# A fused attention and two feed-forward layers: a first-layer result written over its operand, buffers dealt out again, and a new order

## The chip, the core and the metric

The kernel runs on one core of a Trainium2 chip. A core has a matrix engine (TensorE, PE in the profile, with its weight loads as PEld), VectorE (DVE), ScalarE (ACT), GpSimd (POOL) and SyncE (SP), which issues the DMAs. Each engine works through its own queue in order; engines wait for one another by semaphores. The metric is the device time of one execution, in microseconds.

## The reference

`x` is 2 x 12480 x 128, float32. An attention step takes each batch through 32 inducing points; two feed-forward layers without biases follow, each 128 -> 2048 -> 128, over all 24960 tokens:

```
def mab(q, kv): a = softmax(scale * q @ kv.T); return a @ kv
h = mab(inducing, x);  x = mab(x, h)                 # per batch
h = x @ w_in1                                        # first layer
P = a0 + a1*h + a2*h^2 + a3*h^3
Q = 1 + |b0|*|h| + |b1|*h^2
x = (P / (Q + 1e-6)) @ w_out1
h = x @ w_in2                                        # second layer
out = (h * cos(h)) @ w_out2
```

## The kernel before

A first stretch computes the attention weights of both batches, turns the weights to float32, and multiplies the 32 attended rows `h` with `w_in1` (`mst`, `m3`, `m1`), so that the first layer's first product can be had from the attention weights themselves. Then come 52 blocks of 480 tokens. A block has eight first-layer tiles of 256 hidden units, in two halves of 480 columns each, and sixteen second-layer halves of 128 hidden units.

One first-layer tile (`moe1_tile`) goes through these steps; the letters are the names in the code. Per half: `mmA` (TensorE, L847 with `mst`) gives h in a PSUM bank, `sq` (L853) and `ab` (L856) on ScalarE read it, and free the bank. Per tile: `wq` (L859) and `qq` (L862) on GpSimd form Q, `ln` (L865) and `ex` (L868) on ScalarE its inverse, and `ee` (L871) on GpSimd the factor of a Newton step. Per half again: `mmX` (L847 with `m3`), `n1` (L877, VectorE), `mmY` (L847 with `m1`), `gr` (L885, VectorE), `ng` (L890, VectorE), which ends the use of the bank, and `mmB` (L895), which adds the result into `acc[0]`. After a block's last `mmB` one instruction of ScalarE, L951, copies the sum to `xt`: its 52 starts mark the blocks.

A second-layer half (`moe2_tile`) is `mmC` (L978) into a bank, `rk` (L981, ScalarE), `rd` (L984, VectorE), `sn` (L987, ScalarE, a sine), `gg` (L990, VectorE), which frees the bank, and `mmD` (L993) into `acc[1]`. Sine and logarithm need different function tables on ScalarE: L1073 loads one, twice in a block.

Six PSUM banks serve both layers; `hc` limits how many of them the second layer holds. Tiles in SBUF are buffers of kinds `x1` to `x6`, each kind with its own count; one `x1` and one `x2` more lie in the two `wide` tiles. In the first layer `x1` holds |h|, then Q, then `ee`'s result; `x2` holds `wq`, then the inverse; `x3` holds the square; `x4` holds `ng`'s result for `mmB`. The weights are staged in `x4` as they come from DRAM, before the blocks begin.

The order of all engines' queues is made at build time by `Plan.order`: a list scheduler with a cost for each operation (the numbers in `mop(...)`), a number of buffers for each kind, and a due time from the tables `OFF` and `START` (`START` for the first two blocks). An operation that takes a buffer (`acq`) is not placed before an earlier one has given it back (`rel`). On the chip only the order stands; the waits are semaphores.

Of the kernel before, what the change touches and what calls it, by code (L numbers as in the profile page):

```python
# [24 lines left out]


TUNE = {
    "NX": {"x1": 5, "x2": 5, "x3": 5, "x4": 4, "x5": 5, "x6": 6, "hc": 4},
    "PARTS": 1,
    "ADDED": (0, 1, 2, 3, 4, 5, 6, 7),  # L30
    "OFF": {
        "slope1": 0.92, "slope2": 0.28, "shift2": -238.65, "hi": 417.72, "lo": 468.96, "tr": 485.58, "cp": -316.77,
        "kA": 478.1, "kX": 444.49, "kC": -311.86, "mmA": -443.25, "mmX": 423.28, "mmY": 174.81, "mmB": 432.98,
# [3 lines left out]
    },  # L37
    "START": {
        "slope1": 1.67, "slope2": 0.77, "shift2": 13.3, "hi": 39.19, "lo": 476.68, "tr": 416.75, "cp": 442.76,
        "kA": -405.75, "kX": 125.03, "kC": 0.0, "mmA": -197.73, "mmX": 475.77, "mmY": 104.53, "mmB": 57.46,  # L40
        "mmC": 0.0, "mmD": 10.0, "sq": 494.18, "ab": -357.19, "ln": 522.15, "ex": 488.76, "rk": -20.0, "sn": -30.0,
        "wq": -10.71, "qq": 120.95, "ee": 494.63, "wb": -96.93, "n0": 95.71, "n1": -280.16, "gr": 25.55, "ng": 67.25,
        "rd": 0.0, "gg": -10.0, "cpx": 420.38,
    },
}

# [209 lines left out]
def kernel(  # L256
# [13 lines left out]
    NB, N, C = x.shape  # L270
# [7 lines left out]
    TB = G * TP  # L278
# [8 lines left out]
    NX = {k: n for k, n in TUNE["NX"].items() if k != "hc"}  # L287
# [23 lines left out]
    wout1 = const.tile([128, DFF], F32, name="wout1")  # L311
# [12 lines left out]
    acc = [psum.tile([128, 512], F32, name=f"acc{i}") for i in range(2)]  # L324
# [13 lines left out]
    M = {}  # L338
# [103 lines left out]
    def plan_weights(w, out, dst, prio):  # L442

        ends = []
        for f in range(0, DFF, 384):
            n = min(384, DFF - f)
            c, d = {}, {}

            def load(c=c, f=f, n=n):
                raw = M["x4"][c["x4"]][:, 0:2 * n].bitcast(I32)  # L450
                if out:
                    nc.sync.dma_start(out=raw.rearrange("p (k d w) -> p k d w", d=C, w=2), in_=bits_out(w)[:, f // C:(f + n) // C])
                else:
                    nc.sync.dma_start(out=raw.rearrange("p (n w) -> p n w", w=2), in_=bits_in(w)[:, f:f + n, :])

            def tiles(c=c, d=d, n=n):
                raw = M["x4"][c["x4"]][:, 0:2 * n].bitcast(I32).rearrange("p (n w) -> p n w", w=2)
                t = M["x1"][d["x1"]]
                return raw, t[:, 0:n], t[:, n:2 * n]

            ends.append((f, n, plan_narrow(
                n, load, tiles, lambda f=f, n=n: dst[:, f:f + n], prio + 0.05 * len(ends), [],
                acq=[("x4", c, False), ("x1", d, False)], rel=[("x4", c), ("x1", d)],
            )))
        return ends
# [271 lines left out]
    products = {}  # L737
# [47 lines left out]
    def mop(*a, **k):  # L785
        return op(*a, main=True, **k)
# [37 lines left out]
    def moe1_tile(blk, k):  # L824

        b = blk // NQ
        blkd = blocks[blk]
        at = blkd["c"]
        c, ca, cx = {}, [{}, {}], [{}, {}]
        ac = blkd.setdefault("acc1", {})  # L830
# [12 lines left out]
        def hf(kind, h):  # L843
            return fl(kind)[:, h * TB:(h + 1) * TB]
# [4 lines left out]
        def mmA(h):  # L849
            return mm(ca[h], mst, h, start=True, stop=True)  # L850
# [48 lines left out]

# [25 lines left out]
        ng_ = []  # L925
        for h in range(2):
            oX = mop(
                "pe", 205, lambda h=h: mmX(h), [oe, *again, *([blkd["rX"][k]] if h else [])], pri("mmX", h) - 1e5, lock=cx[h],
                acq=[("half", cx[h], False), *([] if h else [("x4", c, True)])], key=pri("kX"),
            )  # L930
            o8 = mop("dve", 600, lambda h=h: n1(h), [oX], pri("n1", h), rel=[("x3", c)] if h else [], lock=cx[h])
            oY = mop("pe", 205, lambda h=h: mmY(h), [o8, *([blkd["rY"][k]] if h else []), blkd.get("Y")], pri("mmY", h) - 1e5, lock=cx[h],
                     rel=[("at", at)] if h and last else [])
            blkd["rX"][k], blkd["rY"][k] = oX, oY
            if h:
                blkd["Y"] = oY
            o9 = mop("dve", 600, lambda h=h: gr(h), [oY, *ng_], pri("gr", h), lock=cx[h], rel=[("x2", c)] if h else [])
            o9 = mop("dve", 600, lambda h=h: ng(h), [o9, o6, *ng_], pri("ng", h), lock=cx[h],
                     rel=[("half", cx[h]), *([("x1", c)] if h else [])])
            ng_ = [o9]  # L940
            prev = mop(
                "pe", 805, lambda h=h: mmB(h), [o9, prev, *within(wout1_ends, 256 * k, 256)], pri("mmB", h),
                acq=[("accB", ac, True)] if k == 0 and h == 0 else [], rel=[("x4", c)] if h else [],
            )
        blkd["B"].append(prev)
        n2_ = prev
# [8 lines left out]
    def moe2_tile(blk, k, h):  # L955
# [154 lines left out]
```

## Time and profile before

| | |
|---|---|
| median of 3 runs | 3115.25 us (3109.82 to 3116.71) |
| profiled execution, its own time | 3111.72 us |
| its span, first to last instruction | 3109.9 us |
| mean granted TensorE clock | 0.966 of full speed |
| busy share: PE, ACT, DVE, POOL | 92%, 90%, 86%, 75% |
| DMA | 48.7 MB, nearly all of it in the first 240 us |

The profile is one execution. A share of the span is a mean over the first stretch and 52 blocks; the blocks are most of it, so that they are read one by one. A duration in a row is from start to end of one instruction; instructions that follow at once overlap a little, so that the start of one to the start of the next is the shorter and better measure of what it costs its engine. An idle time in brackets is that of the engine just before the instruction, with what ended it.

### The profile page before, as it was taken

What the parts mean: (1) busy time and instruction counts of PE and PEld (TensorE: products, weight loads), DVE (VectorE), ACT (ScalarE), POOL (GpSimd) and SP (SyncE); (2) the same over time, 40 slices, a digit from 0 to 9 for tenths busy, and PEclk for the clock granted to TensorE, in tenths of its full rate; (3) what the DMA queues carried; (4) which work ended last, traced back from release to release, by engine and by line L of the source; (5) the groups of instructions that cost most, each with busy time, mean ns of one, the idle gap of its engine ahead of it and who ended that gap; (6) DMA issues with size and microseconds to landing.
All of it is one profiled execution on the core that took longest, in us unless ns stands there. A gap on an engine that the chain in (4) does not pass through costs nothing.

```text
span 3109.9 us, 30950 instructions
## 1 busy us (share of the span) xinstructions
PE 2863.5 (92%) x8903; PEld 1500.0 (48%) x8903; DVE 2676.3 (86%) x4492; ACT 2791.4 (90%) x4701; POOL 2322.5 (75%) x1320
## 2 busy tenths in 40 slices
PE   6669999999999999999998999999989999999998
PEld 3334454554545455454444454544444545455454
DVE  4978898988989888898888898989788989898897
ACT  3558999999999999999899999999898999999995
POOL 0268878787887878878768778787787887878772
PEclk8769999999999999999999999999999999999999
DMA  8420000000000000000000000000000000000000
GB/s 221 141 78 4 4 4 7 4 7 4 7 4 4 7 4 7 4 7 4 4 7 4 4 7 4 4 7 4 7 4 4 7 4 7 4 4 7 4 7 7
DMA packets 27583, 48.73 MB, mean 16 GB/s; under 512 B 3028, under 2 KB 7412, under 8 KB 27412
## 3 DMA queue, kind: packets, MB, share of 16 engines
q1 hardware_dynamic: 27412, 46.76, 5.3%
q8 instruction: 70, 1.15, 0.2%
q14 instruction: 101, 0.83, 0.1%
HBM read 33.97 MB, written 12.78 MB: 15 GB/s over the span
## 4 chain that ended last, share of the span: by engine, by line
PE 35%; ACT 24%; POOL 22%; issue 9%; DVE 8%; DMA 2%; SPq 0%; ACTq 0%; DVEq 0%; POOLq 0%
PE bank L978 15%; PE acc L993 10%; POOL x L871 8%; POOL x L862 7%; PE bank L847 5%; POOL x L859 4%; ACT x L865 4%; PE acc L895 4%; ACT x L868 3%; ACT x L853 3%; ACT x L987 3%; ACT x L856 3%; ACT L1073 2%; ACT x L981 2%; DVE x L890 2%
## 5 line engine op out<-in xcount | busy, mean ns | idle before, releaser
L871 POOL TENSOR_TENSOR x<-x,x 128x960 f32<-128x960 f32 x348 | 779.4, 2246 | 316.6 <-ACT x L868 316.6
L847 PE MATMUL bank<-at,m 128*128 128x480 f32 x1664 | 822.6, 544 | 52.5 <-DVE bank L877 26.7
L895 PE MATMUL acc<-x,wout 128*128 128x480 f32 x1664 | 810.4, 585 | 3.8 <-DVE x L890 2.0
L862 POOL TENSOR_TENSOR x<-x,x 128x960 f32<-128x960 f32 x348 | 781.8, 2252 | 6.5 <-ACT x L856 1.0
L978 PE MATMUL bank<-xt,wt 128*128 128x480 f32 x1664 | 745.5, 578 | 37.9 <-ACT x L856 32.0
L993 PE MATMUL acc<-x,wt 128*128 128x480 f32 x1664 | 770.3, 566 | 0.0
L984 DVE TENSOR_TENSOR x<-x,bank 128x480 f32<-128x480 int32 x832 | 526.5, 649 | 207.2 <-ACT x L981 203.9
L877 DVE SCALAR_TENSOR_TENSOR bank<-bank,par,x 128x480 f32<-128x480 f32 x832 | 580.8, 720 | 55.6 <-PE bank L847 53.8
L859 POOL TENSOR_SCALAR x<-x,babs 128x960 f32<-128x960 f32 x348 | 373.9, 1078 | 313.9 <-ACT x L853 273.7
L981 ACT ACTIVATE x<-bank 128x480 int32<-128x480 f32 x832 | 479.2, 581 | 98.3 <-PE bank L978 94.6
L853 ACT ACTIVATE x<-bank 128x480 f32<-128x480 f32 x832 | 463.8, 590 | 69.3 <-PE bank L847 68.6
L990 DVE TENSOR_TENSOR x<-x,bank 128x480 f32<-128x480 f32 x832 | 512.8, 648 | 6.5 <-ACT x L987 2.4
L847 PEld LDWEIGHTS bank<-at,m 128*128 128x128 f32 x1664 | 309.1, 190 | 433.5 <-DVE bank L877 220.9
L885 DVE SCALAR_TENSOR_TENSOR bank<-bank,par,x 128x480 f32<-128x480 f32 x696 | 490.6, 720 | 26.6 <-PE bank L847 25.0
L847 PE MATMUL bank<-at,mst 128*128 128x480 f32 x832 | 414.1, 547 | 94.3 <-DVE x L890 87.9
L978 PEld LDWEIGHTS bank<-xt,wt 128*128 128x128 f32 x1664 | 313.9, 194 | 385.3 <-issue 149.5
L890 DVE SCALAR_TENSOR_TENSOR x<-x,bank 128x480 f32<-128x480 f32 x696 | 443.4, 649 | 61.1 <-POOL x L871 52.5
L987 ACT ACTIVATE x<-x 128x480 f32<-128x480 f32 x832 | 465.9, 602 | 31.0 <-DVE x L984 28.7
L856 ACT ACTIVATE x<-bank,babs 128x480 f32<-128x480 f32 x696 | 458.5, 697 | 0.0
L895 PEld LDWEIGHTS acc<-x,wout 128*128 128x128 f32 x1664 | 316.2, 194 | 161.0 <-issue 115.6
L993 PEld LDWEIGHTS acc<-x,wt 128*128 128x128 f32 x1664 | 311.8, 189 | 161.2 <-issue 139.7
L865 ACT ACTIVATE x<-x 128x960 f32<-128x960 f32 x348 | 360.8, 1048 | 9.7 <-POOL x L862 8.9
(116 smaller groups left out, 2214.7 us busy)
## 6 DMA issues: line engine op xcount, KB each, us to landing
wide<-in_x_dram SPq DMA_DIRECT2D x75, 240.0 KB, 4.4
out_dram<-on SPq DMA_DIRECT2D x52, 240.0 KB, 2.4
x<-in_x_dram SPq DMA_DIRECT2D x29, 240.0 KB, 7.3
x<-in_moe_w_out_dram SPq DMA_DIRECT2D x10, 384.0 KB, 5.0
x<-in_moe_w_in_dram SPq DMA_DIRECT2D x10, 384.0 KB, 5.3
x<-in_moe_w_out_dram SPq DMA_DIRECT2D x2, 128.0 KB, 4.6
x<-in_moe_w_in_dram SPq DMA_DIRECT2D x2, 128.0 KB, 2.8
ind<-in_inducing_dram SPq DMA_DIRECT2D x1, 16.0 KB, 1.5
```

The lines of the kernel that those rows point to most:

```text
L847: return nc.tensor.matmul(out=ps(e), lhsT=m[k][:, h * 128:(h + 1) * 128], rhs=M["at"][at["at"]], **flags)
L853: nc.scalar.activation(out=hf("x3", h), in_=ps(ca[h]), func=AF.Square)
L856: nc.scalar.activation(out=hf("x1", h), in_=ps(ca[h]), func=AF.Abs, scale=babs[:, 0:1])
L862: nc.gpsimd.tensor_tensor(out=fl("x1"), in0=fl("x2"), in1=fl("x1"), op=ALU.add)
L871: nc.gpsimd.tensor_tensor(out=fl("x1"), in0=fl("x1"), in1=fl("x2"), op=ALU.mult)
L877: nc.vector.scalar_tensor_tensor(out=ps(cx[h]), in0=ps(cx[h]), scalar=par[:, 2:3], in1=hf("x3", h), op0=ALU.add, op1=ALU.mult)
L895: nc.tensor.matmul(out=acc[0][:, 0:TB], lhsT=wout1[:, (2 * k + h) * C:(2 * k + h + 1) * C], rhs=hf("x4", h), start=(k == 0 and h == 0), st ...
L978: return nc.tensor.matmul(out=ps(), lhsT=win2[:, f * 128:(f + 1) * 128], rhs=M["xt"][xc["xt"]], start=True, stop=True)
L981: nc.scalar.activation(out=fl("x5").bitcast(I32), in_=ps(), func=AF.Identity, bias=0.25)
L984: nc.vector.tensor_tensor(out=fl("x5"), in0=fl("x5").bitcast(I32), in1=ps(), op=ALU.subtract)
L987: nc.scalar.activation(out=fl("x5"), in_=fl("x5"), func=AF.Sin, scale=-TWO_PI, bias=0.5 * math.pi)
L993: nc.tensor.matmul(out=acc[1][:, 0:TB], lhsT=wout2[:, f * C:(f + 1) * C], rhs=fl("x6"), start=first, stop=last)
```

## The change

`ng` writes its result over its operand in `x1`; `mmB` reads it there, and `x1` is given back by the second `mmB`, no longer by the second `ng`. `x4` is gone. Its four buffers become two more of `x1` (5 to 7), one of `x2` (5 to 6) and one of `x3` (5 to 6); `hc` goes from 4 to 5. The weights are staged in `x3`. `x2` is taken by `wq` on GpSimd, no longer by `mmA` on TensorE. The planner's costs are set anew, and with them nearly all entries of `OFF` and `START`, of which two lines stand here:

```diff
-    "NX": {"x1": 5, "x2": 5, "x3": 5, "x4": 4, "x5": 5, "x6": 6, "hc": 4},
+    "NX": {"x1": 7, "x2": 6, "x3": 6, "x5": 5, "x6": 6, "hc": 5},
...
-                raw = M["x4"][c["x4"]][:, 0:2 * n].bitcast(I32)
+                raw = M["x3"][c["x3"]][:, 0:2 * n].bitcast(I32)
...
 def ng(h):
-                out=hf("x4", h), in0=hf("x1", h), scalar=-2.0, in1=ps(cx[h]), op0=ALU.add, op1=ALU.mult
+                out=hf("x1", h), in0=hf("x1", h), scalar=-2.0, in1=ps(cx[h]), op0=ALU.add, op1=ALU.mult
 def mmB(h):
-                out=acc[0][:, 0:TB], lhsT=wout1[:, (2 * k + h) * C:(2 * k + h + 1) * C], rhs=hf("x4", h),
+                out=acc[0][:, 0:TB], lhsT=wout1[:, (2 * k + h) * C:(2 * k + h + 1) * C], rhs=hf("x1", h),
...
 # costs: mmA, mmX, mmY 205 -> 213; mmB, mmC, mmD 805 -> 820; n1, gr 600 -> 630; ng 600 -> 570
-                acq=[("half", ca[h], False), *([] if h else [("x1", c, True), ("x2", c, True), ("x3", c, True)])], key=pri("kA"),
+                acq=[("half", ca[h], False), *([] if h else [("x1", c, True), ("x3", c, True)])], key=pri("kA"),
...
-        o3 = mop("pool", 961, wq, sqs, pri("wq"))
+        o3 = mop("pool", 961, wq, sqs, pri("wq"), acq=[("x2", c, True)], key=pri("kA"))
...
-                acq=[("half", cx[h], False), *([] if h else [("x4", c, True)])], key=pri("kX"),
+                acq=[("half", cx[h], False)],
...
-                     rel=[("half", cx[h]), *([("x1", c)] if h else [])])
+                     rel=[("half", cx[h])])
...
-                acq=[("accB", ac, True)] if k == 0 and h == 0 else [], rel=[("x4", c)] if h else [],
+                acq=[("accB", ac, True)] if k == 0 and h == 0 else [], rel=[("x1", c)] if h else [],
```

The work is the same, 6067 instructions of TensorE, 4494 of VectorE, 4689 of ScalarE and 1325 of GpSimd by the built programs' rows; only their order and buffers differ. In both orders a pattern of one block repeats. Before, the order of ScalarE is line for line that of the block ahead in 24 of 50 pairs of neighbouring blocks; after, in 40.

On TensorE, in the middle of a block before, second-layer products (L978, L993) stand among the first layer's (`mst` is `mmA`, `m_76` to `m_83` are `mmX`, `m_84` to `m_91` are `mmY`, `wout` is `mmB`):

```order
L978 MATMUL bank<-xt_137,wt_66 128x480 x2
L847 MATMUL bank<-at_134,m_4_80 128x480
L895 MATMUL acc_97<-x_0_117,wout_67 128x480
L847 MATMUL bank<-at_134,m_4_80 128x480
L895 MATMUL acc_97<-x_0_117,wout_67 128x480
L847 MATMUL bank<-at_134,m_4_88 128x480 x2
L847 MATMUL bank<-at_135,mst_69 128x480
L895 MATMUL acc_97<-x_3_120,wout_67 128x480
L847 MATMUL bank<-at_135,mst_69 128x480
L895 MATMUL acc_97<-x_3_120,wout_67 128x480
L978 MATMUL bank<-xt_137,wt_66 128x480 x4
```

On TensorE after, in the stretch of a block that has most of the second layer; five L978 and the four transposes of L806 stand just ahead of these rows:

```order
L993 MATMUL acc_98<-x_2_128,wt_66 128x480
L978 MATMUL bank<-xt_136,wt_66 128x480 x5
L993 MATMUL acc_98<-x_3_129,wt_66 128x480
L993 MATMUL acc_98<-x_4_130,wt_66 128x480
L993 MATMUL acc_98<-x_5_131,wt_66 128x480
L993 MATMUL acc_98<-x_0_126,wt_66 128x480
L993 MATMUL acc_98<-x_1_127,wt_66 128x480
L993 MATMUL acc_98<-x_2_128,wt_66 128x480
L993 MATMUL acc_98<-x_3_129,wt_66 128x480
L993 MATMUL acc_98<-x_4_130,wt_66 128x480
L993 MATMUL acc_98<-x_5_131,wt_66 128x480
L847 MATMUL bank<-at_134,m_0_76 128x480 x2
```

What moved: 11 of the 16 L978 of a block and 11 of its 16 L993 now stand together, with no first-layer product among them, and the rest of the block is nearly all first layer.

On GpSimd, in a block before (`x_102` to `x_106` and `wide_132` are `x1`, `x_107` to `x_111` and `wide_133` are `x2`, `x_112` to `x_116` are `x3`; L859 is `wq`, L862 `qq`, L871 `ee`):

```order
L859 TENSOR_SCALAR x_3_110<-x_0_112,babs 128x960
L859 TENSOR_SCALAR x_4_111<-x_1_113,babs 128x960
L862 TENSOR_TENSOR x_2_104<-x_3_110,x_2_104 128x960
L862 TENSOR_TENSOR x_4_106<-x_4_111,x_4_106 128x960
L859 TENSOR_SCALAR x_0_107<-x_2_114,babs 128x960
L871 TENSOR_TENSOR wide_132<-wide_132,wide_133 128x960
L862 TENSOR_TENSOR x_3_105<-x_0_107,x_3_105 128x960
L859 TENSOR_SCALAR x_1_108<-x_3_115,babs 128x960
L871 TENSOR_TENSOR x_1_103<-x_1_103,x_2_109 128x960
L862 TENSOR_TENSOR x_0_102<-x_1_108,x_0_102 128x960
L871 TENSOR_TENSOR x_2_104<-x_2_104,x_3_110 128x960
```

On GpSimd after, in a block's second half (`x_102` to `x_108` and `wide_132` are `x1`, `x_109` to `x_114` and `wide_133` are `x2`, `x_115` to `x_120` are `x3`):

```order
L801 TENSOR_TENSOR pk_138<-att_92,pk_138 120x8x32
L871 TENSOR_TENSOR x_0_102<-x_0_102,wide_133 128x960
L871 TENSOR_TENSOR x_4_106<-x_4_106,x_3_112 128x960
L871 TENSOR_TENSOR x_5_107<-x_5_107,x_4_113 128x960
L871 TENSOR_TENSOR x_6_108<-x_6_108,x_1_110 128x960
L859 TENSOR_SCALAR x_0_109<-x_4_119,babs 128x960
L859 TENSOR_SCALAR wide_133<-x_5_120,babs 128x960
L862 TENSOR_TENSOR x_1_103<-x_0_109,x_1_103 128x960
L871 TENSOR_TENSOR x_2_104<-x_2_104,x_5_114 128x960
L862 TENSOR_TENSOR wide_132<-wide_133,wide_132 128x960
L859 TENSOR_SCALAR x_3_112<-x_3_118,babs 128x960
L871 TENSOR_TENSOR x_3_105<-x_3_105,x_2_111 128x960
```

What moved: of the eight L871 of a block, four now stand in one row with no L862 between them; before, at most two did, and two L862 stood ahead of single ones. 160 of the 416 L859 now wait for VectorE, where 91 did.

## Rows read from the trace of the kernel before

**Rows 1.** The page, part 1: busy us, share of the span, number of instructions.

```profile
PE 2863.5 (92%) x8903; PEld 1500.0 (48%) x8903; DVE 2676.3 (86%) x4492; ACT 2791.4 (90%) x4701; POOL 2322.5 (75%) x1320
```

**Rows 2.** Instructions of line 951: durations, first and last start.

```profile
L951 ACT ACTIVATE xt<-acc x52: 571/682/708, 243.4 to 3076.9; 128x480 f32<-128x480 f32 x52
```

**Rows 3.** Timeline of ScalarE: start us, us, line, operation; six of the 52.

```profile
418.27 0.71 ACT L951 ACTIVATE xt<-acc 128x480 f32<-128x480 f32 x1
688.01 0.68 ACT L951 ACTIVATE xt<-acc 128x480 f32<-128x480 f32 x1
1344.29 0.68 ACT L951 ACTIVATE xt<-acc 128x480 f32<-128x480 f32 x1
1698.52 0.68 ACT L951 ACTIVATE xt<-acc 128x480 f32<-128x480 f32 x1
2027.52 0.68 ACT L951 ACTIVATE xt<-acc 128x480 f32<-128x480 f32 x1
2428.16 0.70 ACT L951 ACTIVATE xt<-acc 128x480 f32<-128x480 f32 x1
```

**Rows 4.** Busy time by engine in four stretches (columns in the first line).

```profile
core 0: us, PE busy (x) PEld busy (x) DVE busy (x) ACT busy (x) POOL busy (x), PEclk, DMA share, GB/s
418.30:688.00 269.70, 256.95 (x762) 135.85 (x762) 242.20 (x401) 259.82 (x435) 221.28 (x126) 1.00 0.02 5
489.50:526.10 36.60, 36.60 (x114) 20.08 (x112) 34.78 (x59) 34.72 (x62) 26.97 (x16) 1.00 0.03 7
688.00:743.80 55.80, 53.11 (x154) 27.78 (x152) 48.42 (x81) 52.21 (x89) 44.37 (x26) 0.97 0.02 5
705.50:708.90 3.40, 3.40 (x6) 1.55 (x5) 1.86 (x4) 2.13 (x6) 3.40 (x2) 0.50 0.00 0
```

**Rows 5.** Timelines in one block: idle time and its releaser in brackets.

```profile
481.69 1.88 PE L978 MATMUL bank<-xt,wt 128*128 128x480 f32 x4 [0.74 <-ACT x L856]
487.85 0.48 PE L847 MATMUL bank<-at,mst 128*128 128x480 f32 x1 [1.74 <-DVE x L890]
...
481.70 0.66 DVE L890 SCALAR_TENSOR_TENSOR x<-x,bank 128x480 f32<-128x480 f32 x1 [1.73 <-POOL x L871]
...
476.20 2.24 POOL L862 TENSOR_TENSOR x<-x,x 128x960 f32<-128x960 f32 x1
479.44 2.22 POOL L871 TENSOR_TENSOR x<-x,x 128x960 f32<-128x960 f32 x1
...
474.60 0.99 ACT L868 ACTIVATE x<-x 128x960 f32<-128x960 f32 x1
```

**Rows 6.** Timelines of ScalarE and TensorE: instructions that follow one another at once.

```profile
480.05 1.05 ACT L853 ACTIVATE x<-bank 128x480 f32<-128x480 f32 x2
480.95 1.25 ACT L856 ACTIVATE x<-bank,babs 128x480 f32<-128x480 f32 x2
482.03 1.05 ACT L865 ACTIVATE x<-x 128x960 f32<-128x960 f32 x1
...
506.97 1.59 ACT L987 ACTIVATE x<-x 128x480 f32<-128x480 f32 x3
508.57 1.28 ACT L1073 ACT_TABLE_LOAD   x1
509.87 1.90 ACT L865 ACTIVATE x<-x 128x960 f32<-128x960 f32 x2
511.67 1.89 ACT L868 ACTIVATE x<-x 128x960 f32<-128x960 f32 x2
...
490.30 3.38 PE L978 MATMUL bank<-xt,wt 128*128 128x480 f32 x8
```

**Rows 7.** The page, part 5: groups of instructions.

```profile
L984 DVE TENSOR_TENSOR x<-x,bank 128x480 f32<-128x480 int32 x832 | 526.5, 649 | 207.2 <-ACT x L981 203.9
L877 DVE SCALAR_TENSOR_TENSOR bank<-bank,par,x 128x480 f32<-128x480 f32 x832 | 580.8, 720 | 55.6 <-PE bank L847 53.8
L981 ACT ACTIVATE x<-bank 128x480 int32<-128x480 f32 x832 | 479.2, 581 | 98.3 <-PE bank L978 94.6
```

More of the change, by code (lines that the diff above doesn't have):

```diff
@@ L31 @@
     "OFF": {
-        "slope1": 0.92, "slope2": 0.28, "shift2": -238.65, "hi": 417.72, "lo": 468.96, "tr": 485.58, "cp": -316.77,
-        "kA": 478.1, "kX": 444.49, "kC": -311.86, "mmA": -443.25, "mmX": 423.28, "mmY": 174.81, "mmB": 432.98,
[3 rows of a table removed]
+        "slope1": 0.22, "slope2": 1.13, "shift2": -299.88, "hi": -115.8, "lo": 225.65, "tr": 141.68, "cp": -305.88,
+        "kA": 166.97, "kX": 126.25, "kC": 41.99, "mmA": -91.5, "mmX": 84.49, "mmY": -112.0, "mmB": 415.69,
[3 rows of a table added]
     },
     "START": {
[L39 to L43, printed above, removed]
+        "slope1": 2.42, "slope2": 0.77, "shift2": 13.3, "hi": -268.77, "lo": 278.33, "tr": 53.48, "cp": 50.66,
+        "kA": -204.51, "kX": 102.37, "kC": 0.0, "mmA": -74.63, "mmX": 487.87, "mmY": 141.02, "mmB": 251.0, "mmC": 0.0,
+        "mmD": 10.0, "sq": -289.58, "ab": 199.42, "ln": -89.18, "ex": 151.14, "rk": -20.0, "sn": -30.0, "wq": -687.43,
+        "qq": -122.84, "ee": 279.42, "wb": -96.93, "n0": 95.71, "n1": -84.36, "gr": 66.2, "ng": -739.77, "rd": 0.0,
+        "gg": -10.0, "cpx": 277.38,
     },
@@ L456, in tiles @@
             def tiles(c=c, d=d, n=n):
-                raw = M["x4"][c["x4"]][:, 0:2 * n].bitcast(I32).rearrange("p (n w) -> p n w", w=2)
+                raw = M["x3"][c["x3"]][:, 0:2 * n].bitcast(I32).rearrange("p (n w) -> p n w", w=2)
                 t = M["x1"][d["x1"]]
@@ L462, in plan_weights @@
                 n, load, tiles, lambda f=f, n=n: dst[:, f:f + n], prio + 0.05 * len(ends), [],
-                acq=[("x4", c, False), ("x1", d, False)], rel=[("x4", c), ("x1", d)],
+                acq=[("x3", c, False), ("x1", d, False)], rel=[("x3", c), ("x1", d)],
             )))
@@ L908, in moe1_tile @@
             o = blkd["A"] = mop(
-                "pe", 205, lambda h=h: mmA(h), [blkd["at"], *products[b, k], blkd.get("A"), *(full if blk > 1 else [])],
+                "pe", 213, lambda h=h: mmA(h), [blkd["at"], *products[b, k], blkd.get("A"), *(full if blk > 1 else [])],
                 pri("mmA", h) - 1e5, lock=ca[h],
-                acq=[("half", ca[h], False), *([] if h else [("x1", c, True), ("x2", c, True), ("x3", c, True)])], key=pri("kA"),
+                acq=[("half", ca[h], False), *([] if h else [("x1", c, True), ("x3", c, True)])], key=pri("kA"),
             )
@@ L927, in moe1_tile @@
             oX = mop(
-                "pe", 205, lambda h=h: mmX(h), [oe, *again, *([blkd["rX"][k]] if h else [])], pri("mmX", h) - 1e5, lock=cx[h],
-                acq=[("half", cx[h], False), *([] if h else [("x4", c, True)])], key=pri("kX"),
-            )
-            o8 = mop("dve", 600, lambda h=h: n1(h), [oX], pri("n1", h), rel=[("x3", c)] if h else [], lock=cx[h])
-            oY = mop("pe", 205, lambda h=h: mmY(h), [o8, *([blkd["rY"][k]] if h else []), blkd.get("Y")], pri("mmY", h) - 1e5, lock=cx[h],
+                "pe", 213, lambda h=h: mmX(h), [oe, *again, *([blkd["rX"][k]] if h else [])], pri("mmX", h) - 1e5, lock=cx[h],
+                acq=[("half", cx[h], False)],
+            )
+            o8 = mop("dve", 630, lambda h=h: n1(h), [oX], pri("n1", h), rel=[("x3", c)] if h else [], lock=cx[h])
+            oY = mop("pe", 213, lambda h=h: mmY(h), [o8, *([blkd["rY"][k]] if h else []), blkd.get("Y")], pri("mmY", h) - 1e5, lock=cx[h],
                      rel=[("at", at)] if h and last else [])
@@ L936, in moe1_tile @@
                 blkd["Y"] = oY
-            o9 = mop("dve", 600, lambda h=h: gr(h), [oY, *ng_], pri("gr", h), lock=cx[h], rel=[("x2", c)] if h else [])
-            o9 = mop("dve", 600, lambda h=h: ng(h), [o9, o6, *ng_], pri("ng", h), lock=cx[h],
-                     rel=[("half", cx[h]), *([("x1", c)] if h else [])])
+            o9 = mop("dve", 630, lambda h=h: gr(h), [oY, *ng_], pri("gr", h), lock=cx[h], rel=[("x2", c)] if h else [])
+            o9 = mop("dve", 570, lambda h=h: ng(h), [o9, o6, *ng_], pri("ng", h), lock=cx[h],
+                     rel=[("half", cx[h])])
             ng_ = [o9]
             prev = mop(
-                "pe", 805, lambda h=h: mmB(h), [o9, prev, *within(wout1_ends, 256 * k, 256)], pri("mmB", h),
-                acq=[("accB", ac, True)] if k == 0 and h == 0 else [], rel=[("x4", c)] if h else [],
+                "pe", 820, lambda h=h: mmB(h), [o9, prev, *within(wout1_ends, 256 * k, 256)], pri("mmB", h),
+                acq=[("accB", ac, True)] if k == 0 and h == 0 else [], rel=[("x1", c)] if h else [],
             )
@@ L995, in moe2_tile @@
         oA = mop(
-            "pe", 805, mmC, [blkd["x2"], blkd.get("C"), *(full if blk == 0 else []), *within(win2_ends, 128 * f, 128)], pri("mmC") - 1e5,
+            "pe", 820, mmC, [blkd["x2"], blkd.get("C"), *(full if blk == 0 else []), *within(win2_ends, 128 * f, 128)], pri("mmC") - 1e5,
             acq=[("half", c, False), ("hc", c, True)], rel=[("xt", xc)] if last else [], key=pri("kC") + 0.1 * h, lock=c, tag=t("mmC", -1e5),
@@ L1005, in moe2_tile @@
         m = mop(
-            "pe", 805, mmD, [o4, prev, *within(wout2_ends, 128 * f, 128)], pri("mmD"), acq=[("accD", ac, True)] if first else [],
+            "pe", 820, mmD, [o4, prev, *within(wout2_ends, 128 * f, 128)], pri("mmD"), acq=[("accD", ac, True)] if first else [],
             rel=[("x6", c)], tag=t("mmD"),
```

6 rows, old and new, of the table TUNE are left out of this document.

## The prediction

> **What bounds the kernel now.** First the page's shares: TensorE 92%, ScalarE 90%, VectorE 86% busy [rows 1]. No engine stands out, so the mean says little and I go to the blocks. The starts of line 951 mark them: the first at 243.4, the last, 51 blocks later, at 3076.9 [rows 2]. From 418.27 to 688.01 five blocks take 269.74, or 53.94 each [rows 3]; in them the clock is full and TensorE is idle 12.75 us, 2.55 a block, ScalarE 9.88, 1.98 a block [rows 4]. I call such a block clean. The 51 intervals against 53.94 each:
>
> the first three, 243.4 to 418.27, are 13.1 us too long; the next seventeen, to 1344.29, 9.0; six to 1698.52, 30.6; six to 2027.52, 5.4; seven to 2428.16, 23.1; the last twelve, to 3076.9, 1.4 [rows 2, 3]. So 243.4 + 51 x 53.94 (2750.9) + 82.6 + 33.0 after the last start gives 3109.9, the span. What lies around the span is 1.8 (3111.72 less 3109.9). Three things can be gained: the period of a clean block, the two stretches of 30.6 and 23.1, and the rest of the excess.
>
> Inside one clean block the timelines show a chain. TensorE waits 0.74 us for a bank that `ab` frees, and 1.74 us for one that `ng` frees, at 487.85; `ng` had waited 1.73 us for GpSimd's `ee`, until 481.70. That `ee` started at 479.44, while the `ex` that it needs had ended at 475.59: for nearly 4 us it stood behind L862, L859 and other GpSimd work already queued [rows 5]. These two waits, 2.48, are all but the whole of TensorE's idle 2.55. From 489.5 to the block's end TensorE is busy 36.60 of 36.60 us [rows 4], and there the others wait for it. So the block is one stall that a queue on GpSimd causes, and then a stretch in which TensorE sets the pace.
>
> ScalarE is nearly as full. From start to start `sq` takes 0.45, `ab` 0.54, `ln` and `ex` 0.90, `sn` 0.53 (three before the table load), a table load 1.30 [rows 6]; with `rk` as `sq`, a block's 16 each of `sq`, `ab`, `rk`, `sn`, 16 `ln` and `ex`, two loads and five small copies at 0.45 are 31.5 + 14.4 + 2.6 + 2.2 = 50.7. A block can't be shorter than that.
>
> **The change part by part.** *`ng` in place.* The instruction keeps its engine, size and operands apart from the address; an `n1` that already writes over its operand in the bank is 0.72 [rows 7]. Between an in-place `ng` being free and it costing 16 x 0.07 us a block (0.72 less the 0.65 of `ng` in rows 5), VectorE's idle time covers either: it is busy 242.20 of 269.70, which leaves 5.5 a block [rows 4]. I take nothing.
>
> *Later release of `x1`, `x4` gone.* The next taker of an `x1` is planned behind `mmA`, and `mmB` gives it back, both on TensorE's queue, so the order itself keeps it and no semaphore is added there. A buffer is held longer by one `mmB`, but there are eight with the `wide` one where there were six.
>
> *`x2` taken by `wq`.* This adds waits: 160 `wq` wait for VectorE where 91 did. Behind a waiting `wq` stand `qq` and `ee` on GpSimd, and ScalarE's `ln` waits for these. Its cover is GpSimd's idle time, 269.70 less 221.28, 9.7 us a block [rows 4]; there are seven `x2` for six. If the cover is gone, a `wq` that is late by an `n1` costs 0.72; 69 more of them cost 50 us over the run. I take nothing and keep 0 to 50, since the added places stand in only one or two of eight tiles.
>
> *The order, in a clean block.* On GpSimd four `ee` stand together right behind the table load's `ln` and `ex`, so that those no longer queue behind `qq`; single ones stand behind at most one. On TensorE 22 second-layer products, 11 `mmC` and 11 `mmD`, stand in a run; at no more than 0.85 each (eight passes in 3.38 us, two passes to a product, rows 6) they last up to 18.6 us and need neither `ee` nor `ng`. Four `ee` at 2.24 [rows 5] are 9.0 and fit under it. So the stall of 1.74 should go, and with one more bank allowed to the second layer part of the 0.74. What is late next is ScalarE, at 50.7, and VectorE, whose `rd` already waits 203.9 us in all for `rk` [rows 7]. Bounds: the block can fall to 50.7 (3.2 less), or stay at 53.94 if the stall only moves; or grow (a rival below). I take 52.2, 1.74 less: the one wait that the new order visibly covers, and no more. Times 51 it is 88.7.
>
> *The order, outside the pattern.* The stretches of six blocks (30.6) and seven (23.1) are those where the old order leaves its pattern; at the seam of the two batches extra products have to be made, and there the new order leaves it too, but the second stretch is within the pattern now. I keep 12 of the 30.6 and none of the 23.1: a gain of 41.7. At worst both stay, at best 53.7 goes.
>
> *The clock.* In the block from 688.0 to 743.8 the granted clock is 0.50, 1.2 GHz for 2.4, from 705.5 to 708.9; the block is 55.80, so 1.86 longer [rows 4]. The fall is 17.5 us into the block; TensorE's wait of 1.74 ends about 15.6 into its own (487.85 less 418.27 and one block). The 14.4 us of excess in 23 otherwise regular blocks are then about eight such falls, 0.63 a block. I keep that for 48 blocks, 30, of which 14.4 is there already, because the new order too has places where the matrix engine waits.
>
> The Trainium skill, in "TensorE: Matmul & The Clock Gate", Part 1, says that the clock's gate follows how busy TensorE has been lately, with two levels and none between. The 0.50 behind a wait agrees, but the equal wait in the block of rows 5 went by without a fall; by the rule alone a fall could come in every block or in none, and that is a rival below.
>
> *First stretch and end.* The weights now pass through `x3`, of which four are lent to the transposed `x` at that time, and six pieces come after all of `x`; they are needed only once second-layer work begins. I take nothing, and as bounds the 13.1 of the first three blocks, either way. In the last twelve blocks the excess is 1.4 with falls; taking falls out as counted (12 x 0.63 = 7.6), 6 less is what is left.
>
> **The sum.** 243.4 + 51 x 52.2 (2662.2) + 13.1 + 12 + 30 - 6 + 33.0 = 2987.7, with 1.8 around it 2989.5, against the profiled execution's 3111.72: 122 less. The median of the runs stands 3.5 above that execution, so the forecast is 2993, 3.9% less.
>
> **Rivals.** *The stall moves.* GpSimd's queue still holds single `ee`, and what TensorE no longer waits for it may wait for elsewhere; for it speaks that from 489.5 on TensorE has no idle time left to give; against it that the waits in the order are fewer at that place. Then the period stays at 53.94 and only the stretches gain: 2993 + 88.7 = 3082.
>
> *Both layers run free.* The period falls to ScalarE's 50.7: 2993 - 51 x 1.5 = 2917. For it speaks that only one stall was seen; against it that every `rk` and `sq` would have to find its product ready.
>
> *The clock falls in every block.* 51 x 1.86 = 95 in place of 30: 3058. For it speaks that the stretch outside the run of 22 is nearly all first layer, where each `mmY` needs an `n1`; against it that the long run keeps TensorE busy.
>
> *Slower: VectorE stands between the banks.* A bank goes round in `mmC` 0.85, `rk` 0.58, `rd` 0.65, `sn` 0.53 and `gg`, taken as `rd`, 0.65, some 3.3 us [rows 6, 7]. Five `mmC` take five banks, and the sixth waits for the first one's `gg`. If VectorE's queue has one tile's first-layer work before that `gg`, 2 x (0.72 + 0.72 + 0.65) less overlaps of 0.09, 3.6 us, then TensorE stands for about that long at the run of `mmC`, once a block, with the run's `mmD` queued behind it, and nothing under it as the first layer is elsewhere: 52.2 + 3.6 = 55.8, so 2993 + 184 = 3177. It decides from 2.4 us a block on (122 / 51). For it speaks the 203.9 us that VectorE waited for `rk`, its largest wait; against it that the second layer's VectorE work stands mostly together in the new order.
>
> **How the numbers follow.** Forecast 0.53, stall moves 0.17, both free 0.12, clock 0.05, slower 0.13. The forecast's own range is a period of 51.3 to 53.2, 2947 to 3044. The range for all takes in 3082 with the 13 of the first stretch and part of the late `wq`, and reaches to 2917: 2915 to 3110; outside are the slower rival and about half of the free one's spread. Faster by over 0.2% (6 us, about what a measurement here can tell): all but the slower rival and the upper end of the moved stall, 0.82; within it 0.04; slower 0.14.
>
> **What would show it.** The starts of line 951 come 52.2 apart in most blocks, and no stretch but the seam of the batches leaves that. TensorE's wait for `ng` before an `mmA` is gone; VectorE's wait for `ee` is short. If the period is near 53.9, look for a TensorE wait of 2 us a block with another name: for `gg` it is the slower rival's mechanism at a small price, for `ng` the old one moved. If the clock's mean falls below 0.96 with a clean period, it is the clock. I am wrong if the period is over 53.5, or if the gain comes from before 243.4.

## The result and the profile after

The changed kernel takes 3003.20 us (median of 4 runs, 3001.78 to 3005.75), the one before beside it 3114.04 (4 runs). The ratio is 0.9646, with a 95% interval of 0.9629 to 0.9663. The forecast was 2993 and faster, a ratio of 0.961.

The page of the profile after, part 1 and two groups of part 5 (busy us, mean ns, idle time before and its releaser):

```profile
PE 2859.7 (95%) x8903; PEld 1468.0 (49%) x8903; DVE 2674.0 (89%) x4492; ACT 2752.9 (92%) x4701; POOL 2328.4 (78%) x1320
...
L877 DVE SCALAR_TENSOR_TENSOR bank<-bank,par,x 128x480 f32<-128x480 f32 x832 | 592.5, 719 | 172.2 <-PE bank L847 166.0
L984 DVE TENSOR_TENSOR x<-x,bank 128x480 f32<-128x480 int32 x832 | 514.6, 646 | 36.1 <-ACT x L981 34.2
```

TensorE and ScalarE are 95% and 92% busy, where they were 92% and 90% [rows 1]. `rd` waits 34.2 us for `rk`, which was 203.9 [rows 7]; `n1` now waits 166.0 for TensorE, which was 53.8.

The source view of line 951 after, all 52 of them:

```profile
L951 ACT ACTIVATE xt<-acc x52: 552/589/595, 254.9 to 2967.5; 128x480 f32<-128x480 f32 x52
```

And its timeline, six of them:

```profile
414.83 0.59 ACT L951 ACTIVATE xt<-acc 128x480 f32<-128x480 f32 x1
467.43 0.59 ACT L951 ACTIVATE xt<-acc 128x480 f32<-128x480 f32 x1
678.43 0.59 ACT L951 ACTIVATE xt<-acc 128x480 f32<-128x480 f32 x1
1523.20 0.59 ACT L951 ACTIVATE xt<-acc 128x480 f32<-128x480 f32 x1
1577.08 0.58 ACT L951 ACTIVATE xt<-acc 128x480 f32<-128x480 f32 x1
1653.05 0.59 ACT L951 ACTIVATE xt<-acc 128x480 f32<-128x480 f32 x1
```

From 467.43 to 678.43 four blocks take 211.00, 52.75 each; the blocks from the 7th on are 52.78 to 52.97, with no exception but the seam of the batches and the end. Before, a clean block was 53.94 [rows 3]. The busy time in those four blocks, and in a piece of the seam (PEclk is the granted share of the clock):

```profile
core 0: us, PE busy (x) PEld busy (x) DVE busy (x) ACT busy (x) POOL busy (x), PEclk, DMA share, GB/s
467.40:678.40 211.00, 208.45 (x609) 107.23 (x608) 193.27 (x321) 205.28 (x349) 177.31 (x102) 1.00 0.02 5
1582.20:1595.70 13.50, 9.11 (x15) 4.59 (x16) 7.21 (x13) 13.07 (x21) 10.58 (x6) 0.50 0.00 0
```

TensorE is idle 2.55 us in four blocks, 0.64 in each, where each had 2.55 [rows 4]; ScalarE 1.43 for 1.98. That is 1.91 less idle time of TensorE in a block that is 1.15 shorter: its busy time for the same products reads 52.11 a block, where it was 51.39. Why isn't shown. The clock is full. By the clock's records it was at half for 85 us after the first 300 before; now for 17, all of it at the seam and at the very end.

The source view of line 890 (`ng`) has what `ng` waited for and how long TensorE waited for `ng` (us, times), first before, then after:

```profile
  POOL x L871: 52.5, 69
  POOL wide L871: 8.2, 16
  PE bank L847: 109.7, 65
...
  POOL x L871: 0.4, 2
  PE bank L847: 31.2, 53
```

`ng` no longer waits for `ee`, 0.4 us in all for 60.7. TensorE's waits for `ng` are down to 31.2 us from 109.7; what is left is mostly one wait of 0.52 in each block, before an `mmA`:

```profile
537.24 0.48 PE L847 MATMUL bank<-at,mst 128*128 128x480 f32 x1 [0.52 <-DVE x L890]
```

The chain of the work that ended last, in one block after (start us, us, what):

```profile
548.42 4.03 PE bank L978 x10
...
552.86 0.81 PE bank L978 x2
553.68 1.61 PE acc L993 x4
555.29 4.03 PE bank L978 x10
559.31 7.25 PE acc L993 x18
```

These are the run of 11 `mmC` and 11 `mmD`, two passes to a product: five `mmC` in 4.03, after the transposes one more and two `mmD`, then five `mmC` in 4.03 and nine `mmD` in 7.25. They follow one another without a wait. GpSimd has its one idle stretch of the block meanwhile, and the four `ee` begin as the run ends:

```profile
566.19 2.26 POOL L871 TENSOR_TENSOR x<-x,x 128x960 f32<-128x960 f32 x1 [8.45 <-ACT x L868]
```

Term by term, in the profiled execution's own time:

| term of the sum | forecast | measured |
|---|---|---|
| to the first L951 | 243.4 | 254.9 |
| 51 periods | 51 x 52.2 = 2662.2 | 51 x 52.79 = 2692.3 |
| first three blocks, excess | 13.1 | 414.8 - 254.9 - 158.4 = 1.5 |
| seam of the batches | 12 | 1653.05 - 1523.20 - 105.6 = 24.3 |
| falls of the clock elsewhere | 30 | 0 |
| last blocks | -6 | -5.5 |
| after the last L951, and around the span | 34.8 | 34.3 |
| sum | 2989.5 | 3001.8 |

### The profile page after: what moved, and what is told of

Read it like the earlier page. It is cut to its first block, busy times and chain, and to the rows that moved or that the text cites. A ratio compares the mean times of both kernels' runs of the same rounds, so it can differ in the third digit from the quotient of the medians.

```text
span 3000.0 us, 31085 instructions
## 1 busy us (share of the span) xinstructions
PE 2859.7 (95%) x8903; PEld 1468.0 (49%) x8903; DVE 2674.0 (89%) x4492; ACT 2752.9 (92%) x4701; POOL 2328.4 (78%) x1320
## 3 DMA queue, kind: packets, MB, share of 16 engines
q8 instruction: 70, 1.15, 0.2%
## 4 chain that ended last, share of the span: by engine, by line
PE 71%; DVE 14%; ACT 5%; issue 2%; POOL 1%; DVEq 0%; ACTq 0%; POOLq 0%
PE acc L993 20%; PE bank L978 18%; PE bank L847 16%; PE acc L895 15%; DVE bank L885 4%; DVE x L890 3%; DVE bank L877 3%; DVE x L984 3%; ACT x L865 1%; ACT x L868 1%; PE bank L1019 1%; PE bank L806 1%; ACT x L853 1%; ACT x L856 1%; POOL x L871 1%
## 5 line engine op out<-in xcount | busy, mean ns | idle before, releaser
L871 POOL TENSOR_TENSOR x<-x,x 128x960 f32<-128x960 f32 x311 | 695.6, 2254 | 350.7 <-ACT x L868 350.7
L877 DVE SCALAR_TENSOR_TENSOR bank<-bank,par,x 128x480 f32<-128x480 f32 x832 | 592.5, 719 | 172.2 <-PE bank L847 166.0
L993 PE MATMUL acc<-x,wt 128*128 128x480 f32 x1664 | 730.7, 566 | 0.0
L978 PE MATMUL bank<-xt,wt 128*128 128x480 f32 x1664 | 725.3, 568 | 1.5 <-ACT xt L951 1.2
L895 PE MATMUL acc<-x,wout 128*128 128x480 f32 x1452 | 695.3, 572 | 5.1 <-DVE x L890 3.4
L862 POOL TENSOR_TENSOR x<-x,x 128x960 f32<-128x960 f32 x311 | 696.5, 2253 | 0.8
L984 DVE TENSOR_TENSOR x<-x,bank 128x480 f32<-128x480 int32 x832 | 514.6, 646 | 36.1 <-ACT x L981 34.2
L885 DVE SCALAR_TENSOR_TENSOR bank<-bank,par,x 128x480 f32<-128x480 f32 x714 | 502.6, 717 | 16.6 <-PE bank L847 14.2
L987 ACT ACTIVATE x<-x 128x480 f32<-128x480 f32 x832 | 482.2, 607 | 16.1 <-DVE x L984 15.0
L856 ACT ACTIVATE x<-bank,babs 128x480 f32<-128x480 f32 x726 | 476.9, 698 | 0.0
L978 PEld LDWEIGHTS bank<-xt,wt 128*128 128x128 f32 x1664 | 307.7, 190 | 316.9 <-issue 191.6
L890 DVE SCALAR_TENSOR_TENSOR x<-x,bank 128x480 f32<-128x480 f32 x726 | 456.1, 645 | 7.2 <-DVE bank L885 0.5
L859 POOL TENSOR_SCALAR x<-x,babs 128x960 f32<-128x960 f32 x357 | 391.9, 1105 | 73.8 <-DVE wout L410 47.1
L993 PEld LDWEIGHTS acc<-x,wt 128*128 128x128 f32 x1664 | 315.1, 189 | 257.0 <-issue 239.0
L847 PE MATMUL bank<-at,mst 128*128 128x480 f32 x832 | 344.3, 465 | 53.1 <-DVE x L890 27.0
L868 ACT ACTIVATE x<-x 128x960 f32<-128x960 f32 x357 | 360.0, 1048 | 0.4
L865 ACT ACTIVATE x<-x 128x960 f32<-128x960 f32 x311 | 316.9, 1040 | 16.7 <-POOL x L862 16.3
```

The lines of the kernel that those rows point to most:

```text
L847: return nc.tensor.matmul(out=ps(e), lhsT=m[k][:, h * 128:(h + 1) * 128], rhs=M["at"][at["at"]], **flags)
L856: nc.scalar.activation(out=hf("x1", h), in_=ps(ca[h]), func=AF.Abs, scale=babs[:, 0:1])
L862: nc.gpsimd.tensor_tensor(out=fl("x1"), in0=fl("x2"), in1=fl("x1"), op=ALU.add)
L871: nc.gpsimd.tensor_tensor(out=fl("x1"), in0=fl("x1"), in1=fl("x2"), op=ALU.mult)
L877: nc.vector.scalar_tensor_tensor(out=ps(cx[h]), in0=ps(cx[h]), scalar=par[:, 2:3], in1=hf("x3", h), op0=ALU.add, op1=ALU.mult)
L885: nc.vector.scalar_tensor_tensor(out=ps(cx[h]), in0=ps(cx[h]), scalar=par[:, 0:1], in1=hf("x2", h), op0=ALU.add, op1=ALU.mult)
```

## The experiments

The numbers without an interval are one run each, beside several of the kernel before on the same chip (3108 to 3116); repeated runs of one kernel lay within 0.3%.

### Which part of the change it is: four corners and two more

**New buffers, in-place write and costs, with the old due times** (`OFF` and `START` of before put into the kernel after):

> The new buffers, the in-place write and the new costs, with the due times (OFF, START) of the kernel before. Theory (due times fit one set of buffers): the order has no one-block pattern, TensorE waits for banks in several places, and the block is 54 to 58 us on average; 3080 to 3250 us. Rival (the freed buffers do the work, whatever the due times): 2980 to 3040 us.

Measured: 3730.56 us, 20% more than before and far above the theory's 3250. Blocks of 53 to 58, of about 61 and of about 86 us take turns. Two lines of its page, the span in 40 slices: the busy share of TensorE and its clock, in tenths:

```profile
PE   6758889797897978979778879787879788897878
...
PEclk8768989798997979979788979797979899797979
```

The clock is at half again and again, 0.866 in the mean; it was 0.966.

**Old buffers with `x4`, with the new costs and due times:**

> The old buffers with x4, and the new costs and due times. Theory (due times fit one set of buffers): worse than the kernel before, 54 to 60 us a block; 3120 to 3350 us. Rival (the new due times and costs do the work, the buffers little): 2980 to 3060 us.

Measured: 3165.28 us, 1.8% more than before; most blocks between 54.7 and 57.0 with full clock. That is within the theory's range. So neither the buffers nor these due times bring anything alone, both rivals fall, and the due times are worth 727 us with the new buffers (3730.56 to 3003.20). Due times set anew for the old buffers weren't tried, so it isn't shown that the gain needs the new buffers.

**In place, the freed buffers given to nobody:**

```diff
-    "NX": {"x1": 7, "x2": 6, "x3": 6, "x5": 5, "x6": 6, "hc": 5},
+    "NX": {"x1": 5, "x2": 5, "x3": 5, "x5": 5, "x6": 6, "hc": 4},
```

> The kernel after with its due times and costs and the in-place write, but x4's buffers given to nobody: x1, x2, x3 at 5 each and hc at 4. Theory: longer held x1 with no more of them makes mmA late; slower than the kernel before, 54 to 59 us a block; 3110 to 3300 us. Rival (in place alone is enough): under 3040 us.

Measured: 3265.72 us, blocks of 56.4 to 58.7. It is 100 us longer than the run above, which has the same due times and the same counts of `x1`, `x2`, `x3` and `hc`, but has `x4` too and takes `x2` with `mmA`. So in place without more buffers is slower, as the theory said; that the longer hold of `x1` is the cause is argued and not shown. In place with the old due times and counts wasn't tried.

**The kernel after, planned with the old costs** (205, 805 and three times 600 in place of 213, 820, 630, 630, 570):

> The kernel after, planned with the costs of before (205, 805, 600, 600, 600), its due times and buffers kept. Theory (due times carry the order, the costs only adjust it): a one-block pattern again, 52.5 to 53.5 a block, 2995 to 3040 us. Rival (the durations from the trace are what made the order good): 54 us a block or more, over 3070 us.

Measured: 3057.19 us, between the two. The period is 53.20, so 0.41 more, 21 us of the 54; the first interval (79.2 for 57.9) and the one at the seam (99.0 for 76.0) make 44 more, and a first block that comes 13 us earlier takes some back. The durations from the trace are worth a little in each block and more at the start and at the seam.

### Whether a queued `ee` made TensorE wait before

**Each `ee` of before as early as its `ex` allows:**

```diff
     seq = plan.order()
+    for i in range(len(seq)):
+        if seq[i].fn.__name__ == "ee":
+            j = i
+            while seq[j - 1] not in seq[i].deps and seq[j - 1].fn.__name__ != "ee":
+                j -= 1
+            seq.insert(j, seq.pop(i))
```

> The kernel before, in its own order but for one thing: each ee (L871) stands on GpSimd as early as the ex that it needs allows, so ahead of the qq (L862) and wq that it was queued behind. Theory (the prediction's chain: queued ee, so late ng, so late bank, so a TensorE wait of 1.74 us a block): that wait goes, a clean block falls from 53.94 to 52.2 to 52.8, and with the waits most falls of the clock go; 3010 to 3060 us. Rival 1 (the stall moves): a qq that is 2.25 us later makes ln late, and the block stays at 53.5 to 54.5; 3095 to 3135 us. Rival 2 (the clock falls for another reason): the period shortens but the falls stay, over ten of them after 300 us.

Measured: 3322.86 us, ratio 1.0684 (1.0666 to 1.0702); blocks of 57.4 and 58.7. Worse than either said. The mechanism is that of rival 1, at a higher price: with the `ee` ahead, `qq` is late, and ScalarE's `ln` waits for it, 3.2 us in the block from 560.42, where a block of before has no such wait. The wait view of ScalarE in that block (us, times, longest):

```profile
ACT x L865 <- POOL x L862: 3.2, 2, 2.6
```

So one `ee` alone was moved:

**One `ee` per block, ahead of one `qq` and one `wq`:**

```diff
     seq = plan.order()
+    on_pool = [i for i, o in enumerate(seq) if o.eng == "pool"]
+    for a, b, c, d in zip(on_pool, on_pool[1:], on_pool[2:], on_pool[3:]):
+        if [seq[i].fn.__name__ for i in (a, b, c, d)] == ["qq", "qq", "wq", "ee"] and not any(o in seq[d].deps for o in seq[b:d]):
+            seq.insert(b, seq.pop(d))
```

> The kernel before with one instruction of GpSimd moved per block: where qq, qq, wq, ee stand, the ee goes ahead of the second qq, so it can start 3.3 us earlier; that qq and the wq come 2.25 later, and its ln had 3.6 us to spare in the trace of before. The blunter move of every ee made the blocks 57 to 59 us long. Theory (this one queued ee caused TensorE's wait of 1.74): that wait is gone or under 0.5 and a clean block falls to 52.2 to 53.2; 3040 to 3090 us. Rival (the wait is only the last of several that end at one time; another takes its place): the clean block stays within 0.4 of 53.94, or grows; 3095 to 3140 us.

Measured: 3115.45 us, ratio 1.0008 (0.9999 to 1.0018). The rival holds: the total is that of before, and clean blocks are 54.1 to 54.2. Its timelines on VectorE, GpSimd and TensorE in a block that starts at 473.37:

```profile
481.19 0.65 DVE L890 SCALAR_TENSOR_TENSOR x<-x,bank 128x480 f32<-128x480 f32 x1
484.88 0.65 DVE L984 TENSOR_TENSOR x<-x,bank 128x480 f32<-128x480 int32 x1 [1.73 <-ACT x L981]
488.59 0.65 DVE L890 SCALAR_TENSOR_TENSOR x<-x,bank 128x480 f32<-128x480 f32 x1 [0.51 <-POOL x L871]
...
477.50 2.26 POOL L871 TENSOR_TENSOR x<-x,x 128x960 f32<-128x960 f32 x1
486.31 2.24 POOL L871 TENSOR_TENSOR x<-x,x 128x960 f32<-128x960 f32 x1
...
489.30 0.48 PE L847 MATMUL bank<-at,mst 128*128 128x480 f32 x1 [1.87 <-DVE x L890]
```

The moved `ee` starts 4.13 us into the block, where it stood at 7.2 (479.44 less 418.27 and one block). Its `ng` (481.19) waits no longer, where it waited 1.73 [rows 5]. But `rd`, next on VectorE, waits 1.73 for `rk` instead, and TensorE waits 1.87 for a later `ng`, that of 488.59. This is the one that it waited for before too, as these rows of before show, on VectorE, GpSimd and ScalarE:

```profile
487.14 0.65 DVE L890 SCALAR_TENSOR_TENSOR x<-x,bank 128x480 f32<-128x480 f32 x1 [0.38 <-POOL x L871]
...
484.87 2.23 POOL L871 TENSOR_TENSOR x<-x,x 128x960 f32<-128x960 f32 x1
...
483.38 1.06 ACT L868 ACTIVATE x<-x 128x960 f32<-128x960 f32 x1
```

The bank that TensorE wanted at 487.85 [rows 5] came from this `ng`, not from that of 481.70. Its `ee` began at 484.87, 0.4 us after its `ex` had ended. The busy time from the start of this block of before to 489 (PE, PEld, DVE, ACT, POOL):

```profile
472.10:489.00 16.90, 14.42 (x40) 6.83 (x39) 13.51 (x22) 16.85 (x27) 16.90 (x10) 1.00 0.01 1
```

ScalarE worked 16.85 and GpSimd 16.90 of 16.90 us there. Whatever the order in a queue without a pause, what stands behind all of it comes no sooner. That this sets the length of the stretch is an argument from busy times.

### What sets the pace now

Five kernels are the kernel after with the same order and part of the work left out, so that an engine has less to do: three with one part, two with two. The period is one run's median block. On the chip of the first three the kernel of the next section, whose clean blocks have the order of the kernel after, has 52.76, so what they save isn't the chip's doing.

**Half of `ln` and `ex`:** `hf("x2", 0)` and `hf("x1", 0)` in place of `fl("x2")` and `fl("x1")`, 480 of 960 columns.

> The kernel after, same order, with ln and ex on the first 480 of 960 columns only (half of that work is left out): ScalarE has 16 x 0.4, some 6.4 us less a block. Theory (TensorE now sets the pace, its idle 0.64 of 52.79): the period falls by less than 1.2 us, to 51.6 to 52.8. Rival (ScalarE's path sets it): 48 to 50.5 us.

Measured: 2981.32 us, the period 52.38, as the theory said. Four blocks of it (window, PE, PEld, DVE, ACT, POOL busy, clock):

```profile
517.50:727.00 209.50, 206.95 (x609) 107.91 (x608) 192.77 (x321) 183.12 (x349) 177.05 (x101) 1.00 0.02 5
```

**Half of `rd`**, 240 of 480 columns:

> The kernel after, same order, with rd (L984) on 240 of 480 columns (that half is left out): VectorE has 16 x 0.25, 4 us less a block. Theory (VectorE is not the bound, it waits 3.6 us a block for TensorE): the period falls by less than 0.6. Rival (VectorE stands between the banks, the slower rival's mechanism at a small price): the period falls by 1 to 2.5.

Measured: 2988.58 us, the period 52.51, as the theory said. Four blocks:

```profile
520.90:731.00 210.10, 205.80 (x610) 108.32 (x609) 181.29 (x321) 204.96 (x350) 177.19 (x102) 1.00 0.02 5
```

**Half of `mmD` in 14 of 16:**

```diff
-            nc.tensor.matmul(out=acc[1][:, 0:TB], ..., rhs=fl("x6"), start=first, stop=last)
+            n = TB if first or last else TB // 2
+            nc.tensor.matmul(out=acc[1][:, 0:n], ..., rhs=fl("x6")[:, 0:n], start=first, stop=last)
```

> The kernel after, same order, with the second layer's last product (L993) on 240 of 480 columns in 14 of 16 halves (that half of the work is left out): TensorE has 14 x 0.4, 5.6 us less a block. Theory (TensorE sets the pace): the period falls by 1.5 to 3, until ScalarE's 50.7 binds: 50 to 51.3. Rival (TensorE is only full because it is waited into shape, another engine sets the pace): 52.3 to 52.8.

Measured: 3025.49 us, so 22 more than with the whole work. Two neighbouring blocks:

```profile
524.40:576.80 52.40, 48.42 (x153) 26.54 (x152) 48.16 (x80) 51.33 (x89) 44.31 (x26) 0.99 0.02 5
576.80:630.20 53.40, 49.40 (x153) 27.50 (x153) 48.34 (x80) 51.47 (x89) 44.21 (x26) 0.98 0.02 5
```

The first is 52.4; the other is 53.4 with a lower clock, and later every block is 54.6. The mean granted clock is 0.950, with the whole work it was 0.975. The theory's 50 to 51.3 falls, and the rival's 52.3 to 52.8 is what the blocks with a nearly full clock show. TensorE waits 7.6 us in these two blocks, 4.8 for VectorE and 2.8 for ScalarE, where two blocks of the kernel after have 1.0. The two largest (us, times, longest):

```profile
PE bank L847 <- DVE bank L877: 3.8, 6, 1.0
PE bank L1020 <- ACT ot L1016: 1.6, 2, 0.8
```

Yet the rival's reason isn't right either:

**Half of `ln`, `ex` and `rd` together:**

> The kernel after, same order, with half of ln and ex and half of rd left out, together; alone they took 0.4 and 0.3 us off a block of 52.79. Theory (TensorE has a floor of its own near 52: weight loads and changes between kinds of product on top of the 49.5 of work): 51.8 to 52.3, TensorE idle under 0.5 a block. Rival (no engine but a chain through several of them sets the pace): 50 to 51.5.

Measured: 2945.27 us, the period 51.65, between what theory and rival said; TensorE's idle time, 0.43 a block, is as the theory said. Four blocks:

```profile
515.80:722.30 206.50, 204.78 (x609) 108.40 (x608) 180.63 (x321) 182.08 (x348) 177.08 (x101) 1.00 0.02 5
```

**Half of `ln`, `ex` and `mmD` together:**

> The kernel after, same order, with half of ln and ex, and of 14 of 16 L993, left out. TensorE lightened alone took 0.3 us off a block whose clock stayed up, ScalarE alone 0.4. Theory (both are at their floors, so each alone hides the other): blocks with full clock fall by 2 to 4, to 48.5 to 51. Rival (VectorE's chain is next at once): over 51.5. TensorE has less to do, so falls of the clock as with it alone (35 after 300 us) are expected in either case.

Measured: 2834.41 us, the period 49.42, as the theory said. The falls of the clock that were expected don't come: it is 0.976 in the mean. Four blocks:

```profile
508.20:705.80 197.60, 189.28 (x609) 106.76 (x608) 191.96 (x321) 183.15 (x348) 176.97 (x101) 1.00 0.02 6
```

Alone, the lighter ScalarE takes 0.4 off a block and the lighter TensorE 0.4; together they take 3.4. Both are near their floors in this order at the same time: TensorE near 51.65 (ScalarE and VectorE lightened, 1.7 us idle in 206.5), ScalarE near 52.4 (TensorE lightened, 1.1 us idle in the block of 52.4). The kernel after is 52.79, 0.4 above the higher one. These are floors of the order, not of the work: the same products read 208.45 us busy in four blocks of the kernel after and 204.78 here. TensorE and VectorE lightened together wasn't run.

### The seam

```diff
-                    plan_product(s // NQ, k, ready_h[s // NQ], 16.0 * s - 8.0 + OFF["slope1"] * k, win1_ends)
+                    plan_product(s // NQ, k, ready_h[s // NQ], 16.0 * s - 1000.0 + OFF["slope1"] * k, win1_ends)
```

> The kernel after, with the second batch's products (the tables mst, m3, m1) due 992 units earlier, so that the planner takes each as soon as the last block of the first batch has let its table go. The seam of the batches costs 24 us above two clean blocks there, 14 of it with the clock at half. Theory (the products come late because they are due late, and the first layer of the new batch starves): the seam costs 8 to 16, total 8 to 16 us less than the kernel after, 2987 to 2996 us. Rival (the tables are free only once the old block is through, so that the due time changes nothing): within 3 us of the kernel after. Rival (they push other work aside): 5 to 20 us slower.

Measured: 3061.10 us (3059.34 to 3063.07), 58 more than the kernel after. Slower, as the last rival said, but far over its size. The block after the seam takes 125.3, where it was 76.0; its busy time:

```profile
1578.50:1703.80 125.30, 84.86 (x170) 37.28 (x168) 59.10 (x94) 67.72 (x115) 62.15 (x36) 0.66 0.01 2
```

The clock is 0.66 in the mean of this window: it was at half for 85 us on end. The products didn't come earlier. Seven of the eight stand at 1563 to 1579 (the kernel after has all eight at 1562 to 1577), and the eighth comes 79 us later than there. TensorE's last L745, first after, then here, and the L751 behind it:

```profile
1576.54 0.59 PE L745 MATMUL bank<-win,hT 128*128 128x256 f32 x2
...
1655.48 1.22 PE L745 MATMUL bank<-win,hT 128*128 128x256 f32 x2 [1.50 <-DVE x L890]
...
1656.74 0.38 ACT L751 ACTIVATE mst<-bank 128x256 fp32r<-128x256 f32 x1 [44.65 <-PE bank L745]
```

ScalarE's queue stands 44.65 us for it. Why the planner put the eighth so late isn't shown, and none of the three accounts has it. None of the seven kernels here that do all of the work beats the kernel after.

## Why the prediction was right, and where it wasn't

*The direction and the size.* Right, by the case held likeliest: the period is 52.79, in its 51.3 to 53.2, and 3003 is in its 2947 to 3044. The gain is 3.5%, forecast 3.9%.

*The stretches outside the pattern.* Right. The order's rows said that only the seam leaves the pattern, and the starts of line 951 show it: the seven blocks that cost 23.1 extra are gone. The seam was mis-sized: 24.3, where 12 was kept.

*The period.* 52.2 was forecast, by a reason that fell; 52.79 was measured, so that 1.15 us a block came of the 1.74. The step that failed is the chain inside a clean block: `ng` had waited 1.73 us for a queued `ee`, and this was put down as the cause of TensorE's 1.74. With that `ee` moved, `ng`'s wait went and TensorE's stayed, 1.87. The two waits of equal length were 6 us apart, on different `ng`. What the rows of before show in its place is a block in two parts: up to 489, ScalarE and GpSimd work without a pause (16.85 and 16.90 of 16.90 us) and TensorE loses its 2.5 us; from 489.5 TensorE has none, 36.60 of 36.60 [rows 4], and ScalarE loses its 2. In the new order neither part is left: TensorE's idle 0.64 and ScalarE's 1.43 are what remains, and the lightened kernels show both engines near their floors. That GpSimd or ScalarE set the first part's length before is read from busy times; no run lightened them there. Nor do the four `ee` fit under the run of 22, as was forecast: they begin at 566.19, as the run ends, since the `ex` that the first of them waits for comes that late. `ng` has no wait for `ee` all the same, and TensorE's waits for `ng` went as forecast; what in the new order took them away isn't shown.

*The floor.* ScalarE's 50.7 was taken as a bound for a block. It is the sum of start-to-start times; with TensorE lightened the block was still 52.4, with ScalarE busy 51.33 of it. In this order the case "both run free" (2917) was out of reach.

*The clock.* 30 us were kept for falls and none came outside the seam. The rival with a fall in each block (3058) fell too. The theory of the falls was too simple: it looked at a wait of 1.74, which the new order hasn't got; that a wait of such a size was what made the clock fall isn't shown by itself, but in `pe_light` (half of `mmD`) only TensorE's work was cut, and the clock fell, and with ScalarE cut as well it did not. The rule in the Trainium skill, in "TensorE: Matmul & The Clock Gate", Part 1, that the gate follows how busy TensorE has been lately agrees: TensorE was busy 208.45 of 211.00 us in the kernel after and 189.28 of 197.60 with both cut, without a fall, and 48.42 of 52.40 in `pe_light`, where falls came.

*The slower rival.* It didn't come. TensorE's `mmC` run stands without a wait in the chain, and `rd`, which was to be late, waits 34.2 us in all.

*Costs at nothing.* `ng` in place is free: L890 takes 639 to 657 ns before and 636 to 656 after, and the groups of `n1` and `rd` keep their durations (719 and 646 ns; 720 and 649 in rows 7). `wq`'s added waits: GpSimd's idle time is one stretch of 8.5 us per block, before an `ee`, and none before `wq`. The staging in `x3`: the first block is 11.5 us later, but with the old buffers, staged in `x4`, and the new due times and costs it starts at 254.7 too, and with the new buffers and costs and the old due times at 224.9. So the due times and not the staging did it, together with the costs, since with the old costs it starts at 241.8.

The errors nearly cancel: period 30, seam 12 and start 11.5 too low, clock 30 and first blocks 11.6 too high. That the total came within 12 us (3001.8 for 2989.5) is in part luck.

## What to carry to other kernels

Where a planner sets the order, due times and buffer counts are one setting: of this change, the due times without the buffers made the kernel 1.8% slower, the buffers without the due times 20%. Two waits of the same length in one block are not yet a chain: find which instance released which, and move one instruction before believing it. Where two engines are both near their floors, lightening either shows next to nothing, so lighten them in pairs.

## What the runs showed of the hardware

Less work for TensorE made the kernel slower: with 14 of 16 `mmD` halved, 3025 us for 3003, and a granted clock of 0.950 for 0.975. TensorE then waited 7.6 us in two blocks for VectorE and ScalarE, where it had waited 1.0. With ScalarE cut as well the same lighter TensorE kept its clock (0.976) and the time was 2834.
